# Channel products by halves with seven products (Strassen) in a second part, three pair streams, two fold buffers and plain blocks of 128 rows

## The chip, the cores and the metric

One core of one Trainium2 chip. The metric is the device time of one execution in microseconds, median of several. The profile is one execution with the hardware profiler on; its span is 1.8 us shorter than the time of that same execution (1486.8 against 1488.62 before) and some 5 us below the medians. The granted clock is the share of TensorE's full clock that it was given, as the profile shows it. TensorE is called PE below, VectorE DVE, ScalarE ACT, GpSimd POOL, SyncE SP.

## The reference

```python
# attention: q, k, v of (8, 8, 576, 64), omega (128, 64)
phi(x) = exp(x @ omega.T - |x|^2 / 2 - rowmax) / sqrt(128)
num    = phi(q) @ (phi(k).T @ v);  den = phi(q) . sum(phi(k)) + 1e-6
x      = num / den, heads side by side         # (8, 576, 512)
# Fourier mixing and channel products
u   = x + real(fft(fft(x, axis=1), axis=2))
un  = (u - mean) / sqrt(var + 1e-6)            # over the last axis
out = u + relu(un @ w_ch1) @ w_ch2             # 512 -> 2048 -> 512
```

All of it is float32 (the weights arrive as float64). There are 4608 rows of 512.

## The kernel before

The program is a set of streams (generators) whose steps name an engine, an assumed duration, what they wait for and which buffers they take. A list scheduler runs them against a model of the engines before anything runs on the chip, and so fixes the order of instructions on every engine. On the chip each engine works through its own list in that order and waits where its data are not there. Two pair streams do the attention of two heads each, `mixing` does the Fourier part of a batch, `channels` the two channel products. All run in one list, so the channel products fill TensorE's gaps in the first 700 us; work that does so is called filler below.

```python
def folds(n, which, dur, **more):            # n = 0 on VectorE, 1 on GpSimd
    yield Step(which, dur[0], **more)        # more: take=("half",)
    eng, op = ((nc.vector, ALU.add), (nc.gpsimd, ALU.subtract))[n]
    h = fft.tile([CP, NC3, DM], F32, name="half", tag="half")    # one buffer
    eng.tensor_tensor(out=h[:], in0=lo, in1=hi, op=op)
    ...                                      # three more operations
    yield Step(which, 0.2, makes=("fold", b, n), give=("half",))
...
yield from folds(0, DVE, (1.8, 1.0, 0.56), take=("half",))
yield Fork(folds(1, POOL, (3.5, 1.85, 1.1), take=("half",)))
...                                          # yp: y takes "half" too
def pairs(start):
    for n in range(start, B * NP, 2):
        if n >= 3 * NP:
            yield Step(NONE, late=PACE)      # 25 us
        yield from attn(n)
...
Listing(buffers).run([first(), loads(), norms(), mixing(),
                      pairs(0), pairs(1), channels(), weights()])
```

In the profiles `pp`, `kvp`, `tps`, `ndp` are TensorE's attention work, `yp` and `ab` its Fourier work, `tp` the transposes of the normed rows, `hp` and `op` the first and second channel product. `kq` and `vd` are loads of k, q and v; `half` and `fold` the folds ahead of `yp` (VectorE adds rows and columns of x to their mirror images, GpSimd subtracts them); `nmx` and `e` the softmax.

## Time and profile before

| | before |
|---|---|
| time, median | 1491.95 us (1490.35 to 1494.24, 4 runs) |
| TensorE busy | 1413.0 of 1486.8 us |
| channel products, of that | 1008.6 us |
| up to 697.7 us (all streams mixed) | TensorE busy 627.5, idle 70.2 |
| after 697.7 us | channel products only, 83.79 us for 384 rows |

The table of stretches tells where TensorE waits. Its columns are the stretch, its length, busy time of PE, PE load, DVE, ACT and POOL with instruction counts, the granted clock, the DMA share and GB/s.

```profile
0.00:250.00 250.00, 190.95 (x1333) 156.88 (x1334) 160.03 (x327) 118.85 (x348) 93.94 (x105) 0.88 0.58 160
250.00:697.70 447.70, 436.58 (x2723) 320.13 (x2722) 182.80 (x446) 182.88 (x564) 97.17 (x98) 0.99 0.39 104
697.70:1486.80 789.10, 785.45 (x2189) 407.26 (x2187) 56.06 (x126) 84.06 (x170) 15.21 (x24) 1.00 0.08 28
```

From 250 us on TensorE is hardly ever idle.

### The profile page before, as it was taken

What the parts mean: (1) busy time and instruction counts of PE and PEld (TensorE: products, weight loads), DVE (VectorE), ACT (ScalarE), POOL (GpSimd) and SP (SyncE); (2) the same over time, 40 slices, a digit from 0 to 9 for tenths busy, and PEclk for the clock granted to TensorE, in tenths of its full rate; (3) what the DMA queues carried; (4) which work ended last, traced back from release to release, by engine and by line L of the source; (5) the groups of instructions that cost most, each with busy time, mean ns of one, the idle gap of its engine ahead of it and who ended that gap; (6) DMA issues with size and microseconds to landing.
All of it is one profiled execution on the core that took longest, in us unless ns stands there. A gap on an engine that the chain in (4) does not pass through costs nothing.

```text
span 1486.8 us, 16157 instructions
## 1 busy us (share of the span) xinstructions
PE 1413.0 (95%) x6241; PEld 884.3 (59%) x6241; DVE 398.9 (27%) x898; ACT 385.8 (26%) x1081; POOL 206.3 (14%) x226
## 2 busy tenths in 40 slices
PE   8666888899999999999999999999999999999999
PEld 7555666677777777766454545455454545555453
DVE  6756585534344353513100101010100101010000
ACT  7543534435344544321010101111010101111010
POOL 3334354221203030322000000000000000000000
PEclk9878989999999999999999999999999999999999
DMA  8745634444433535222101001010101001010101
GB/s 220 189 126 157 180 93 137 129 118 119 112 100 97 137 82 148 60 64 75 50 0 46 19 29 36 15 50 9 56 0 39 25 29 36 15 50 6 37 0 36
DMA packets 133987, 108.60 MB, mean 73 GB/s; under 512 B 99236, under 2 KB 99492, under 8 KB 133910
## 3 DMA queue, kind: packets, MB, share of 16 engines
q1 hardware_dynamic: 127766, 86.06, 21.2%
q0 software_dynamic: 6144, 21.50, 4.5%
q8 instruction: 50, 0.82, 0.2%
q14 instruction: 27, 0.22, 0.0%
HBM read 79.22 MB, written 33.03 MB: 75 GB/s over the span
## 4 chain that ended last, share of the span: by engine, by line
PE 80%; DMA 11%; DVE 3%; POOL 2%; issue 2%; ACT 1%; SPq 1%; DVEq 0%; POOLq 0%; ACTq 0%
PE hp L724 31%; PE op L747 31%; PE pp L398 5%; PE kvp L420 3%; DMA x<-xb 3%; DMA xb<-xs 2%; PE tps L337 2%; PE yp L555 2%; DMA raw<-in_moe_w_ch_dram 2%; PE ndp L457 1%; DMA xs<-xo 1%; PE ab L581 1%; PE tp L681 1%; DVE half L515 1%; ACT e L366 1%
## 5 line engine op out<-in xcount | busy, mean ns | idle before, releaser
L747 PE MATMUL op<-w,ht 128*128 128x512 f32 x1152 | 505.7, 593 | 0.0
L724 PE MATMUL hp<-unT,w 128*128 128x384 f32 x1536 | 502.9, 486 | 0.0
L724 PEld LDWEIGHTS hp<-unT,w 128*128 128x128 f32 x1536 | 289.7, 190 | 197.4 <-issue 4.3
L747 PEld LDWEIGHTS op<-w,ht 128*128 128x128 f32 x1152 | 215.3, 190 | 248.5 <-issue 244.9
L710 ACT ACTIVATE ht<-hp 128x384 f32<-128x384 f32 x188 | 92.5, 492 | 683.4 <-PE hp L724 683.4
L761 DVE TENSOR_TENSOR ur<-ur,op 128x512 f32<-128x512 f32 x36 | 24.7, 687 | 711.2 <-PE op L747 711.2
L366 ACT ACTIVATE e<-pp,nmx 128x128 f32<-128x128 f32 x576 | 154.8, 421 | 108.1 <-DVE nmx L354 108.0
L398 PE MATMUL pp<-om,kqT 128*128 128x256 f32 x576 | 142.9, 400 | 34.2 <-DVE xo L472 13.3
L398 PEld LDWEIGHTS pp<-om,kqT 128*128 128x128 f32 x576 | 112.8, 201 | 60.7 <-issue 19.1
L675 POOL TENSOR_TENSOR rstd<-rstd,mhalf 128x1 f32<-128x1 f32 x36 | 23.0, 645 | 657.2 <-DVE rstd L673 657.2
L354 DVE TENSOR_REDUCE nmx<-pp 128x4 f32<-128x512 f32 (+1 forms) x160 | 95.9, 631 | 65.8 <-PE pp L398 54.4
L420 PE MATMUL kvp<-vd,e 128*128 128x130 f32 x576 | 82.0, 300 | 7.8 <-ACT e L366 6.9
L420 PEld LDWEIGHTS kvp<-vd,e 128*128 128x128 f32 x576 | 79.5, 212 | 15.2 <-ACT e L366 10.1
L515 POOL TENSOR_TENSOR half<-x 97x1536 f32<-97x1536 f32 x8 | 28.5, 3565 | 207.3 <-DVE rden L468 138.7
L286 POOL TENSOR_TENSOR w<-w,raw 128x512 f32<-128x512 f32 x32 | 44.0, 1380 | 95.3 <-DVE raw L284 82.5
L343 ACT ACTIVATE kqT<-tps 128x512 f32<-128x512 f32 (+1 forms) x96 | 42.5, 510 | 42.5 <-PE tps L337 42.2
L343 ACT ACTIVATE qeT<-tps 128x512 f32<-128x512 f32 (+1 forms) x96 | 41.1, 512 | 33.5 <-PE tps L337 33.5
L457 PE MATMUL ndp<-kv,qeT 128*64 128x65 f32 x1152 | 41.0, 227 | 7.9 <-DVE kv L432 7.6
L457 PEld LDWEIGHTS ndp<-kv,qeT 128*64 128x64 f32 x1152 | 36.9, 140 | 19.4 <-issue 17.7
L337 PE MATMUL tps<-ident,kq 128*128 128x128 f32 x288 | 42.2, 284 | 6.0 <-DMA kq<-in_k_dram 3.6
L685 ACT ACTIVATE unT<-tp 128x512 f32<-128x512 f32 x36 | 19.5, 601 | 99.8 <-PE tp L681 99.8
L604 DVE SCALAR_TENSOR_TENSOR bmp<-ab,bmp 97x65 f32<-97x65 f32 x96 | 25.0, 326 | 71.2 <-ACT bmp L599 70.2
(59 smaller groups left out, 750.4 us busy)
## 6 DMA issues: line engine op xcount, KB each, us to landing
raw<-in_moe_w_ch_dram POOLq DMA_DIRECT2D x32, 512.0 KB, 5.1
kq<-in_k_dram SPq DMA_DIRECT2D x32, 288.0 KB
kq<-in_q_dram SPq DMA_DIRECT2D x32, 288.0 KB
vd<-in_v_dram SPq DMA_DIRECT2D x64, 144.0 KB
xs<-xo SPq DMA_DIRECT2D x64, 144.0 KB
out_dram<-ur SPq DMA_DIRECT2D x36, 256.0 KB
u<-us SPq DMA_DIRECT2D x32, 256.0 KB
ur<-us SPq DMA_DIRECT2D x32, 256.0 KB
```

What stands on the lines that cost most here:

```text
L286: nc.gpsimd.tensor_tensor(out=dst, in0=dst, in1=lof, op=ALU.add)
L337: nc.tensor.transpose(ps[:, (j - j0) * 128 : (j - j0 + 1) * 128], src(j), ident[:])
L343: nc.scalar.activation(out=dst[:, j0:j1, :].rearrange("q c p -> q (c p)"), in_=ps[:, 0 : 128 * (j1 - j0)], func=AF.Copy,)
L354: nc.vector.tensor_reduce(nmx[:, 0:num], ps[:, 0 : MF * num].rearrange("p (c m) -> p c m", m=MF), axis=AX.X, op=ALU.max, negate=True,)
L366: nc.scalar.activation(out=e[:, c, :], in_=ps[:, MF * c : MF * c + MF], func=AF.Exp, bias=nmx[:, c : c + 1],)
L398: nc.tensor.matmul(ps[:, 256 * j : 256 * j + 256], lhsT=kqT[:, 2 * t + j, :], rhs=om2[:].rearrange("p i m -> p (i m)"),)
L420: nc.tensor.matmul(kvp[:, 0 : 2 * (D + 1)], lhsT=feature(r), rhs=vds[n % NV][:, r, :], start=(r == 0), stop=(r == R - 1),)
L457: nc.tensor.matmul(ndp[r // 5][cols, (D + 1) * (r % 5) : (D + 1) * (r % 5 + 1)], lhsT=qeT[:, r, cols], rhs=kvs[0][:, i, :],)
L515: eng.tensor_tensor(out=h[:], in0=lo, in1=hi, op=op)
L710: nc.scalar.activation(out=ht[:], in_=hp[:], func=AF.Relu)
L724: nc.tensor.matmul(hp[:], lhsT=w1[:, dc, 128 * fc : 128 * fc + 128], rhs=unTs[j][:, dc, :], start=(dc == 0), stop=(dc == NDC - 1),)
L747: nc.tensor.matmul(yp[:], lhsT=hs[fc][:, 128 * i : 128 * i + 128], rhs=w2[:, fc, :], start=(fc == 0), stop=(fc == NFC - 1),)
```

## The change

The intent is to save an eighth of the channel products. With each operand cut in halves, seven products and some additions replace eight products. The sums of the weights need memory, so the program is cut in two. In the first part run attention, Fourier part and 512 plain rows. In the second, with its own buffers, run the other 4096 rows in eight blocks of 512.

```diff
+    NS = 3                       # pair streams
     NV = 2                       # load buffers for k, q and for v
-    TB = 384
+    NHALF = 2                    # buffers for the folds and for y
+    TP = 128
+    NPLAIN = 4                   # plain blocks of 128 rows, first part
+    TB = 512                     # rows of a late block
...
-            h = fft.tile([CP, NC3, DM], F32, name="half", tag="half")
+            h = fft.tile([CP, NC3, DM], F32, name="half", tag="half", bufs=NHALF)
...
-    def pairs(start):
-        for n in range(start, B * NP, 2):
-            if n >= 3 * NP:
-                yield Step(NONE, late=PACE)
-            yield from attn(n)
+    def pairs(start):
+        for n in range(start, B * NP, NS):
+            yield from attn(n)
...
+    listing.run([first(), loads(), plain_norms(), mixing()]
+                + [pairs(i) for i in range(NS)] + [plain(), weights()])
+    early.close()                # the first part's memory is free
...
+    # first layer, one column group: seven products in three banks
+    product(x, lambda d: w1[:, d, f], lambda d: un[:, d, t1], True)
+    yield Fork(save("p1", x))                      # ACT copies the bank
+    product(z, lambda d: w1s[:, 0, d, f], lambda d: tt[:, 0, d, :], True)
+    yield Fork(save("p5", z))
+    product(x, lambda d: w1s[:, 1, d, f], lambda d: tt[:, 1, d, :], False)
+    ...                                            # four more
+    # relu of a sum on DVE (a custom add with clamping), sums hs on POOL
+    # second layer: the same scheme, sums added to the residual on DVE
+    listing.run([late_norms(), halves(), weight_sums()])
```

## The prediction

> **What bounds the kernel now.** I read the page's busy row and slices first, then the chain of waits in order of time, then the TensorE timeline of the steady part and of the mixed part, then the table of stretches.
>
> ```profile
> PE 1413.0 (95%) x6241; PEld 884.3 (59%) x6241; DVE 398.9 (27%) x898; ACT 385.8 (26%) x1081; POOL 206.3 (14%) x226
> ...
> PE   8666888899999999999999999999999999999999
> ...
> PEclk9878989999999999999999999999999999999999
> ...
> L747 PE MATMUL op<-w,ht 128*128 128x512 f32 x1152 | 505.7, 593 | 0.0
> L724 PE MATMUL hp<-unT,w 128*128 128x384 f32 x1536 | 502.9, 486 | 0.0
> ```
>
> TensorE (PE) is the bound. The two channel products take 505.7 + 502.9 = 1008.6 us of its 1413.0, with no idle time before them; VectorE and ScalarE are at a quarter. Only the first slices show a PE that waits.
>
> ```profile
> 697.71 32.62 PE op L747 x76
> 730.33 41.28 PE hp L724 x128
> 771.61 8.58 PE op L747 x20
> 781.50 32.62 PE op L747 x76
> ```
>
> In the chain of waits (start, duration, what) everything from 697.71 us on is channel work, 83.79 us for each 384 rows. The spacing of matmuls is 41.28/128 = 0.3225 us at 384 columns and 8.58/20 = 0.429 at 512: columns times 0.833 ns plus 2.5 ns. Each product written in the kernel is two such instructions.
>
> ```profile
> 408.19 4.05 PE L398 MATMUL pp<-om,kqT 128*128 128x256 f32 x18
> 412.07 2.18 PE L420 MATMUL kvp<-vd,e 128*128 128x130 f32 x18
> 414.09 2.75 PE L724 MATMUL hp<-unT,w 128*128 128x384 f32 x8
> ```
>
> These are the decisive lines, as the change makes all late products 256 wide. Starts are 3.88 us apart for 18 matmuls of 256 columns with weights loaded for each: 0.2156 us, again 256 x 0.833 + 2.5. Even 130 columns go at 2.02/18 = 0.112 us. So narrow matmuls keep the full rate, though one weight load is listed at 190 to 212 ns: loads overlap one another and the matmuls.
>
> ```profile
> 0.00:50.00 50.00, 36.29 (x290) 32.00 (x291) 29.84 (x64) 29.66 (x87) 16.45 (x29) 0.93 0.84 219
> 50.00:100.00 50.00, 33.56 (x279) 29.33 (x277) 28.75 (x56) 24.41 (x76) 11.57 (x11) 0.81 0.56 153
> 100.00:150.00 50.00, 36.91 (x260) 31.12 (x259) 37.24 (x85) 21.79 (x66) 23.29 (x25) 0.84 0.51 143
> 150.00:200.00 50.00, 40.69 (x237) 30.55 (x237) 31.71 (x52) 22.47 (x67) 20.94 (x17) 0.87 0.51 139
> 200.00:250.00 50.00, 43.51 (x273) 33.89 (x272) 32.47 (x75) 20.52 (x57) 21.68 (x24) 0.93 0.47 143
> ```
>
> Columns: PE, PE load, DVE, ACT, POOL busy, granted clock, DMA share, GB/s. PE idles 13.7 + 16.4 + 13.1 + 9.3 + 6.5 = 59 us here, at a clock of 0.81 to 0.93; from 250 us to the end it idles only some 12 more. What holds it, in the lists of waits of DVE (50 to 100 us), ACT (100 to 150) and PE (0 to 100); columns: total, times, longest:
>
> ```profile
> DVE half L515 <- DMA x<-xb: 12.9, 1, 12.9
> ...
> ACT e L366 <- DVE nmx L354: 14.6, 1, 14.6
> ...
> PE pp L398 <- DVE xo L472: 11.4, 1, 11.4
> ```
>
> These are one event near 84 to 99 us: DVE stands on a transfer for the Fourier part; the softmax behind it in the same queue stands too, and PE behind that.
>
> **What the Trainium skill says.** "FP8 and Floating Point Precision" under "TensorE Precision Notes" lists true FP32 as four passes through the array (H*H + H*L + L*H + L*L); the trace agrees: two instructions a product at 0.833 ns a column, which is two passes each at the 2.4 GHz of the TensorE page. "TensorE: Matmul & The Clock Gate", Part 1, "What's actually happening", says an idle window of about 3.4 us drops the clock to half; the granted 0.81 to 0.93 where PE waits, against 1.00 later, agrees. The same page under "Architectural detail: the array is 16× 32×32, not 1× 128×128" calls ACT and DVE strict FIFO; the 12.9 us wait above, passed on to the softmax, agrees. "SBUF — State Buffer", "SBUF: two separate sides", says of the port shared by VectorE and GpSimd that a two-SBUF-input VectorE operation and a GpSimd one that reads SBUF block each other. The change puts many such pairs side by side; no run here isolates it yet.
>
> **The change, part by part.** Rows 512 to 4607 (8 blocks of 512) move to a second part that starts when all attention and Fourier work is done. Each product is split in halves: seven products for eight.
>
> Late products. First layer per block: 8 column groups x 7 products x 2 matmuls = 112; second layer: 2 x 7 x 8 = 112. In 8 blocks 1792, each 2 x 0.2156 = 0.4313 us: 773 us. Before, these rows cost 82.48 us per 384 rows without transposes, so 880 us. Gain 107 us, one eighth.
>
> Their side work, per pair of column groups (2 x 14 x 0.4313 = 12.1 us of PE): ACT 8 evictions of 256 columns at about 0.39 us (289 columns take 417 ns) = 3.1; DVE 6 adds at 0.42 (estimate from 687 ns at 512) = 2.5; POOL 8 additions at 0.74 (257 columns take 744 ns) = 5.9. All lie beside PE. A product waits for the eviction of the one before it in the same bank, but the order of instructions puts two others, 1.7 us, between them, against about 0.9 us of drain, semaphores and copy. I allow 3 us for all seams, and 112 late transposes x 0.11 = 12 us.
>
> First part. It keeps 512 rows as blocks of 128: 256 products of 128 columns x 2 x 0.109 = 56 us, and 64 of 512 columns x 2 x 0.429 = 55 us: 111, what these rows cost before too. The other work of this part I take from the kernel before: up to 697.7 us PE carried 384 hp instructions (124 us) and 1152 - 76 - 9 x 96 = 212 op instructions (91), 215 us, and idled 70; so all else took 697.7 - 215 - 70 = 412 us. (At full clock it would be 32 pairs x 9.07 + 8 Fourier stages x 10 + transposes = 375; the clock costs the rest.) Then 412 - 3 + 111 = 520, plus idle time. The start idles as before, 59 us: those waits are queues standing on DMA and a third stream stands with the others. Later, filler is 111 us where it was 215, and the deliberate pacing of pairs is gone, so the transfers of the Fourier part are less covered: 25 instead of 12. First part: 520 + 84 = 604 us. (DVE and ACT have some 325 and 290 us to do in it, so they are not the bound.)
>
> Boundary. The order of instructions shows sixteen transposes (four tiles) behind the last plain product, then the first late one, which needs the last of four differences on DVE. DVE, in order behind the last plain addition: seven weight sums (7 x 0.69 = 4.8), statistics of two tiles (2.05, by 0.69 + 0.18 + 0.15 each), POOL's power, the scaling (0.54), then the other two tiles, whose loads wait for the first tiles' buffers (about 4.5 us from issue, as for u before), with sums in between, then four differences (2.8). Laid end to end: first tiles normed at 11 to 13 us after the last plain product, second loaded at 16 to 17, normed at 22, differences at 26. So 27 us with 1 to 3 us for a cold clock.
>
> End: last addition and store, 4 us as now (1483.2 to 1486.8).
>
> Sum: 604 + 27 + 773 + 12 + 3 + 4 = 1423 us of span; timed runs stand 5 us above the profiled span (1491.7 against 1486.8): 1428.
>
> **The rivals.** First: the late products do not reach 0.2156. Each group is only four instructions with a semaphore ahead, and weights alternate between tables. At 0.23 it costs 1792 x 2 x 0.0144 = 52 us, and the time is 1480. Against it: pp also waits on semaphores every four instructions and holds the rate. For it: POOL and DVE share a port, and hs from POOL gates the second layer; yet POOL has 5.9 of 12.1 us and 6.9 us of other products to catch up in.
>
> Second: the first part becomes a chain of latencies. With little filler, PE may idle 130 us instead of 84, about 1475. For it: DVE's waits on x sum to 60.9 us over the kernel, mostly hidden behind channel products that are now gone. Against: three streams give the list more to place there.
>
> Third: three streams and the missing pacing do better than I allow, and idle falls to 45 us: 1390.
>
> Fourth: the boundary is wider, since late tiles take over early memory and must wait for its last readers and transfers: the order shows the first late load waiting on all queues. 45 us instead of 27: 1446.
>
> **Range and chances.** The 107 us of the products are near certain if the rate holds; 27 go to the boundary, 3 to seams, 13 to idle time of a first part with less filler: 64 remain, 4%. The uncertainty is mostly the idle time of the first part (plus or minus 30) and the boundary (plus or minus 10): 1392 to 1465. Faster by over 2% means under 1461.9: 0.85; within 2%: 0.12; slower: 0.03.
>
> **What would show it.** The late part should run 98 to 99 us per 512 rows (against 111.7 before), with matmuls of 256 columns 0.216 us apart and PE busy throughout; the last plain product should end near 604 us, with one PE gap of about 25 us behind it whose releaser is DVE; POOL should be near half busy in the first layer, without PE waiting on it. I am wrong on the rate if the late part takes over 830 us, and on the first part if it ends outside 570 to 640.

## The result, and the profile after

The changed kernel is correct and slower: 1535.48 us median (1532.04 to 1539.56, 4 runs) against 1491.95. The ratio is 1.0292 (95% interval 1.0261 to 1.0322). Ratios here are the mean time of one kernel's runs over that of the other's runs of the same rounds, so not quite the ratio of the medians. The predicted 1428 and its range of 1392 to 1465 were wrong.

The page of the changed kernel, its busy row and two rows of slices (38 us each):

```profile
PE 1333.8 (87%) x7777; PEld 1153.0 (75%) x7777; DVE 594.3 (39%) x1254; ACT 405.2 (26%) x1189; POOL 402.1 (26%) x482
...
PE   6656886687968859667799999999999999999999
...
PEclk8869988898989979789899999999999999999999
```

TensorE has 79 us less to do (1413.0 to 1333.8), yet the span grew by 43. The low digits, which ended in the eighth slice before, now go on into the twentieth. Stretches of the changed kernel, to be set against those of before:

```profile
0.00:250.00 250.00, 184.34 (x1407) 160.66 (x1407) 150.25 (x300) 117.80 (x358) 83.34 (x90) 0.85 0.54 146
250.00:719.00 469.00, 358.24 (x2658) 297.20 (x2658) 226.90 (x457) 170.02 (x543) 122.58 (x104) 0.88 0.37 98
719.00:760.00 41.00, 24.43 (x107) 20.39 (x107) 31.52 (x61) 7.77 (x18) 8.51 (x12) 0.79 0.25 75
760.00:1530.20 770.20, 766.77 (x3608) 674.76 (x3606) 185.59 (x437) 109.66 (x270) 187.64 (x276) 1.00 0.09 30
```

Between 250 and 719 us TensorE is idle for 469 - 358 = 111 us, and its clock is 0.88 where it was 0.99. From 760 us on it is idle for 3 us, which is the end.

The late part is as planned. Two starts of a block, one block apart, in the TensorE timeline:

```profile
839.21 1.03 PE L901 MATMUL sx<-unT,w 128*128 128x256 f32 x4
...
937.66 1.03 PE L901 MATMUL sx<-unT,w 128*128 128x256 f32 x4
```

That is 98.45 us for 512 rows, where 83.79 us for 384 rows had made 111.7 before. The first late product starts at 738.92 us, where the prediction had 604 + 27 = 631. From there to the last matmul's end it takes 788 us, and 788 had been predicted (773 + 12 + 3). So the whole error of 107 us in the span lies ahead of the first late product.

The boundary, in the TensorE timeline (the last plain product ends at 719.1):

```profile
717.67 1.45 PE L769 MATMUL op<-w,ht 128*128 128x512 f32 x3
729.26 2.02 PE L688 MATMUL tp<-ident,u 128*128 128x128 f32 x8 [10.14 <-DVE u L684]
736.96 2.17 PE L688 MATMUL tp<-ident,u 128*128 128x128 f32 x8 [5.67 <-DVE u L684]
738.92 2.64 PE L901 MATMUL sx<-unT,w 128*128 128x256 f32 x8
741.40 0.81 PE L901 MATMUL sz<-tt,w1s 128*128 128x256 f32 x3
```

It takes 20 us, not 27. TensorE waits for VectorE's scaling of the rows (u), as foreseen, but the first product (sx) needs only the transposed rows; sz is the first that uses the differences.

What TensorE waited for in the changed kernel (us in total, times, longest):

```profile
PE yp L567 <- DVE fold L538: 48.1, 5, 15.9
PE tps L349 <- DMA kq<-in_k_dram: 36.0, 7, 18.2
PE yp L567 <- DVE nmx L366: 29.3, 3, 16.0
PE tp L688 <- DVE u L684: 28.6, 5, 11.5
PE kvp L432 <- DMA vd<-in_v_dram: 23.4, 5, 13.2
```

Before, yp waited for 0.6 us in all. Now it waits for 48.1 + 29.3 = 77, and everything behind it in TensorE's order waits too. The folds of one batch show why. First before, then after (start, duration, what):

```profile
94.22 1.76 DVE L515 TENSOR_TENSOR half<-x 97x1536 f32<-97x1536 f32 x1 [12.94 <-DMA x<-xb]
96.01 0.95 DVE L517 TENSOR_TENSOR half<-half 97x765 f32<-97x765 f32 x1
97.00 1.03 DVE L526 TENSOR_TENSOR fold<-half 97x384 f32<-97x384 f32 x2
97.95 0.16 DVE L534 COPY mid<-half 97x3 f32<-97x3 f32 x1
...
98.20 3.42 POOL L515 TENSOR_TENSOR half<-x 97x1536 f32<-97x1536 f32 x1 [20.37 <-DVE rden L468]
```

```profile
95.97 1.76 DVE L527 TENSOR_TENSOR half<-x 97x1536 f32<-97x1536 f32 x1 [0.31 <-DMA x<-xb]
96.02 5.01 POOL L527 TENSOR_TENSOR half<-x 97x1536 f32<-97x1536 f32 x1 [18.95 <-DMA x<-xb]
97.77 4.07 DVE L529 TENSOR_TENSOR half<-half 97x765 f32<-97x765 f32 x1
...
101.10 2.40 POOL L529 TENSOR_TENSOR half<-half 97x765 f32<-97x765 f32 x1
101.87 3.31 DVE L538 TENSOR_TENSOR fold<-half 97x384 f32<-97x384 f32 x2
103.58 2.46 POOL L538 TENSOR_TENSOR fold<-half 97x384 f32<-97x384 f32 x2
...
105.11 0.96 DVE L546 COPY mid<-half 97x3 f32<-97x3 f32 x1
```

With one buffer GpSimd begins when VectorE has ended. With two, both begin at 96.0 and take turns. GpSimd's first operation lasts 5.01 us for 3.42, as VectorE's first 1.76 us go ahead of it. VectorE's second then stands until GpSimd's ends at 101.03, and ends 0.8 us later, about its own length. VectorE is held 10.1 us instead of 3.9 in each of eight batches, while GpSimd's folds end 10.3 us after the data are there instead of 11.9. The durations agree with the exclusive lock of "SBUF — State Buffer", "SBUF: two separate sides": whichever operation starts first has the shared port pair for the whole instruction. The prediction cited that section for the second part, where it did little harm (VectorE's custom additions took at most 0.425 us; of GpSimd's 256 sums one took 1.05 us, the others at most 0.73), and did not apply it to the folds.

### The profile page after: what moved, and what is told of

Its sections match the earlier page's. It is cut to its first block, busy times and chain, and to the rows that moved or that the text cites. A ratio compares the mean times of both kernels' runs of the same rounds, so it can differ in the third digit from the quotient of the medians.

```text
span 1530.2 us, 20250 instructions
## 1 busy us (share of the span) xinstructions
PE 1333.8 (87%) x7777; PEld 1153.0 (75%) x7777; DVE 594.3 (39%) x1254; ACT 405.2 (26%) x1189; POOL 402.1 (26%) x482
## 4 chain that ended last, share of the span: by engine, by line
PE 70%; DMA 13%; DVE 8%; SPq 3%; issue 3%; ACT 2%; POOL 1%; DVEq 0%; POOLq 0%
PE sx L988 14%; PE sx L901 14%; PE sz L988 7%; PE sz L901 7%; PE sy L988 4%; PE yp L567 4%; PE sy L901 3%; PE pp L410 3%; DMA x<-xb 3%; PE kvp L432 3%; DMA xs<-xo 2%; PE tps L349 2%; DMA xb<-xs 2%; PE hp L746 2%; DVE half L529 2%
## 5 line engine op out<-in xcount | busy, mean ns | idle before, releaser
L961 POOL TENSOR_TENSOR hs<-ht,ht 128x256 f32<-128x256 f32 x64 | 46.7, 729 | 455.6 <-DVE ht L888 455.6
L915 ACT ACTIVATE s<-sx 128x256 f32<-128x256 f32 x128 | 49.2, 384 | 328.0 <-PE sx L901 328.0
L901 PE MATMUL sx<-unT,w 128*128 128x256 f32 x512 | 131.8, 381 | 0.0
L567 PE MATMUL yp<-cs_sb,fold 97*128 97x289 f32 x96 | 45.9, 657 | 81.8 <-DVE fold L538 48.1
L988 PE MATMUL sx<-w,ht 128*128 128x256 f32 x512 | 114.4, 379 | 0.0
L901 PEld LDWEIGHTS sx<-unT,w 128*128 128x128 f32 x512 | 97.9, 191 | 13.4
L988 PEld LDWEIGHTS sx<-w,ht 128*128 128x128 f32 x512 | 96.7, 190 | 12.9
L432 PEld LDWEIGHTS kvp<-vd,e 128*128 128x128 f32 x576 | 78.3, 211 | 34.9 <-issue 23.5
L567 PEld LDWEIGHTS yp<-cs_sb,fold 97*128 97x128 f32 x96 | 29.4, 319 | 95.8 <-issue 34.3
L349 PEld LDWEIGHTS tps<-ident,kq 128*128 128x128 f32 x288 | 36.7, 155 | 46.2 <-issue 41.3
L901 PE MATMUL sx<-tt,w 128*128 128x256 f32 x256 | 65.7, 380 | 0.8 <-DVE ht L888 0.8
```

Of the source, the lines that this page charges most:

```text
L349: nc.tensor.transpose(ps[:, (j - j0) * 128 : (j - j0 + 1) * 128], src(j), ident[:])
L432: nc.tensor.matmul(kvp[:, 0 : 2 * (D + 1)], lhsT=feature(r), rhs=vds[n % NV][:, r, :], start=(r == 0), stop=(r == R - 1),)
L567: nc.tensor.matmul(yp[:, 0:NK], lhsT=fold[:, c, n, :], rhs=tab[:, c, :], start=(c == 0), stop=(c == NC3 - 1),)
L901: nc.tensor.matmul(ps[:, 0:HT], lhsT=left(dc), rhs=right(dc), start=start and dc == 0, stop=(dc == D2 - 1), skip_group_check=True,)
L915: nc.scalar.activation(out=s[:], in_=ps[:, 0:HT], func=AF.Copy)
L961: nc.gpsimd.tensor_tensor(out=o, in0=l, in1=r, op=op)
```

## The experiments

The first set of theories was:
- Collision: the two fold buffers cost, by the lock and by the place in the order that the list, which assumes no collision, gives to yp.
- Streams: the third pair stream costs.
- Filler: the channel products of before had covered waiting that nothing covers now.

The runs in one table. The last two columns are from the profiles: start of the first late product, and TensorE's idle time ahead of it. Rounds of one kernel before differed a little (medians 1491.95 to 1497.1), so the ratio is the safer number.

| run | time, us | ratio to before (95%) | first late product, us | idle ahead, us |
|---|---|---|---|---|
| the change | 1535.5 | 1.029 (1.026, 1.032) | 738.9 | 192 |
| half1 | 1485.3 | 0.993 (0.989, 0.997) | 689.5 | 154 |
| honest | 1524.3 | 1.020 (1.018, 1.022) | 729.2 | 183 |
| yown | 1501.9 | 1.006 (1.002, 1.009) | 708.1 | 162 |
| ns2 | 1502.4 | 1.006 (1.003, 1.009) | 709.1 | 163 |
| ns2_half1 | 1467.5 | 0.980 (0.977, 0.984) | 676.3 | 131 |
| ns2_half1_pace | 1463.2 | 0.978 (0.975, 0.980) | 674.4 | 133 |
| ns2_half1_pace_hold | 1464.4 | 0.980 (0.976, 0.983) | 675.9 | 125 |
| half1_kq3 | 1507.7 | 1.009 (1.007, 1.011) | 710.3 | 174 |
| half1_nv3 | 1480.9 | 0.990 (0.988, 0.993) | 687.3 | 146 |
| half1_nv3_p8 | 1485.0 | 0.994 (0.991, 0.997) | 788.8 | 132 |
| ns2_half1_pace_p8 | 1445.0 | 0.967 (0.965, 0.969) | 745.4 | 95 |
| ns2_half1_p8 | 1443.6 | 0.964 (0.961, 0.967) | 752.9 | 106 |
| ns2_half1_pace_p12 | 1457.6 | 0.977 (0.971, 0.982) | 863.1 | 97 |
| b_late | 1611.4 | 1.079 (1.075, 1.083) | 602.1 | 155 |

In the runs with p8 and p12 more rows are done ahead of the first late product, so their starts are not to be compared with the others. In b_late it is the first channel product. All gave the right result.

**One fold buffer (half1).**

```diff
-    NHALF = 2
+    NHALF = 1
```

> The changed kernel with one buffer for the half folds instead of two, so that VectorE's and GpSimd's folds run one after the other again. Collision theory (the two folds block each other, 10.1 us on VectorE instead of 4.0, and the order list, which counts on 4.1, puts the Fourier matmuls about 8 us too early, in front of everything else on TensorE; 77 us of TensorE idle time in front of yp): VectorE's fold is back at 4 us, idle time before yp under 20 us, time 1455 to 1480. Streams theory (three pair streams on two load buffers, 59 us of waiting on kq and vd): within 10 us of the changed kernel's 1535. Filler theory (the gaps were always there, the removed channel products had filled them): within 20 us of 1535, the idle time moving from yp to other lines.

It gave 50 us, from 1535.5 to 1485.3. VectorE's folds are short again; one group of half1 (busy us, mean ns, idle before):

```profile
L529 DVE TENSOR_TENSOR half<-half 97x765 f32<-97x765 f32 x8 | 7.6, 954 | 0.2
```

This one took 4055 ns on average in the changed kernel. The waits of TensorE in half1 no longer name yp, except for 2.0 us, but those on the loads of k stay:

```profile
PE tps L349 <- DMA kq<-in_k_dram: 44.6, 9, 18.8
...
PE kvp L432 <- DMA vd<-in_v_dram: 11.5, 4, 7.6
```

The time came out 5 us above the expected 1455 to 1480, so of the 77 us in front of yp 50 came out in the time. Streams and filler had both expected about 1535 and missed. The collision theory holds for a large part of the loss, not for all.

**True durations for the list (honest), and a buffer of its own for y (yown).** One buffer changes two things: the folds follow each other, and y, which shares their buffers, must wait for the second fold, so that yp is listed later. These two runs try to take them apart; yown also changes y's buffer in the list, in lines left out here.

```diff
-        yield from folds(0, DVE, (1.8, 1.0, 0.56), take=("half",))
-        yield Fork(folds(1, POOL, (3.5, 1.85, 1.1), take=("half",)))
+        yield from folds(0, DVE, (1.8, 4.05, 1.7), take=("half",))      # honest
+        yield Fork(folds(1, POOL, (4.9, 2.4, 1.25), take=("half",)))
```

> The changed kernel with two fold buffers, but the durations that the order list assumes for the folds set to what the trace shows (VectorE 1.8, 4.05, 1.7, 1.7; GpSimd 4.9, 2.4, 1.25, 1.25). The collision stays, only the order of instructions changes. Collision theory, in its part about the order: the Fourier matmuls come later in TensorE's order, idle time before yp falls from 77 us to under 35, time 1475 to 1505. If the collision costs only by holding VectorE, no change (1525 to 1540). Streams and filler theories: 1520 to 1540.

```diff
-    NHALF = 2
+    NHALF = 1                                                           # yown
...
-                y = fft.tile([128, 4, NK], F32, name="y", tag="half", bufs=NHALF)
+                y = fft.tile([128, 4, NK], F32, name="y", tag="y", bufs=1)
```

> The changed kernel (three streams) with the folds back in one buffer, but the Fourier products' result y in a buffer of its own. Only the folds' running at the same time is taken away; the second buffer stays for y. If it is the collision: as half1, 1475 to 1490. If half1 gained because y's reuse of the buffer put yp in a better place: over 1500.

With true durations and the collision kept, 1524.3: 11 us, not the 30 to 60 expected. With the collision gone and yp free to be listed early, 1501.9, between the two outcomes. Taken at face value, some 34 of half1's 50 us come from the end of the collision (1535.5 to 1501.9) and some 17 from the later place of yp that the shared buffer enforces (1501.9 to 1485.3). This split is a reading and not shown, as each edit rearranges the whole list. In yown yp still waits 42 us:

```profile
PE yp L567 <- DVE fold L538: 25.3, 5, 11.4
PE yp L567 <- DVE nmx L366: 16.7, 2, 10.5
```

**Two streams (ns2, ns2_half1), and the old hold on the pairs (ns2_half1_pace).**

```diff
-    NS = 3
+    NS = 2
...
         for n in range(start, B * NP, NS):
+            if n >= 3 * NP:                     # only in ns2_half1_pace
+                yield Step(NONE, late=25.0)
             yield from attn(n)
```

> The changed kernel with two pair streams instead of three (two fold buffers stay). Streams theory: the waits on kq and vd (59 us) fall to under 15 us, time 1480 to 1495. Collision theory: those waits only follow from the late Fourier matmuls; time 1520 to 1550 and the idle time before yp stays above 50 us. Filler theory: longer, 1540 to 1570, as there is less work to put in the gaps.

> Two pair streams and one fold buffer, without the holding back of pairs. If the two costs found (50 us for two fold buffers, 33 us for three streams) add up, 1455 to 1470, and the holding back is worth nothing (under 10 us against ns2_half1_pace at 1463). If the holding back of pairs was what helped there, 1480 or more.

> The first part as the kernel before has it (two streams, one fold buffer, each pair from the twelfth on held back 25 us in the order list), with only the 512 plain rows to fill it. Filler theory: it is the removed filler that costs; the first part keeps its old length of about 690 us although 100 us of channel work is gone from it, time 1500 to 1530. Collision theory: the first part ends near 600 to 620 us and the time is 1430 to 1450.

Two streams are better by 33 us with two fold buffers and by 18 with one. In the same way one fold buffer is worth 50 us with three streams and 35 with two: the two costs overlap. No theory had foreseen ns2: streams expected 1480 to 1495, collision 1520 to 1550 and filler 1540 to 1570, and 1502 came out. Collision's yp waits did stay, at 43.5 + 27.8 us in ns2. The hold is worth nothing measurable (1463 against 1467). Most important, with both edits undone the time is still 1463, between the 1430 to 1450 of the collision theory and the 1500 to 1530 of the filler theory. Something is left that none of the edits undone here carries.

**The kernel before without its filler (b_late).** This edits the kernel before, not the changed one.

```diff
     def channels():
+        yield Step(NONE, after=(("us", B - 1),))      # all Fourier work done
         for j in range(NTB):
             yield from mlp(j)
```

> The kernel before with nothing of the change in it, except that its channel products start only when all attention and Fourier work is done: the first part without any filler. It measures what the prediction took from the sums of the kernel before, 412 us of other work plus idle time. If my 84 us of idle time for the first part were right for the pattern of waits and only the change's own edits spoiled it, the first part is 480 to 510 us and the time 1495 to 1525. If the channel products had hidden far more waiting than the profile of before showed as idle, the first part is 530 us or more and the time 1545 or more.

The time is 1611.4 us and the first channel product starts at 602.1. The stretches of b_late:

```profile
0.00:250.00 250.00, 176.26 (x1336) 152.97 (x1337) 153.44 (x321) 120.65 (x364) 88.02 (x100) 0.84 0.62 166
250.00:602.12 352.12, 271.29 (x2087) 233.35 (x2086) 165.69 (x391) 155.50 (x496) 91.17 (x86) 0.86 0.43 108
```

Attention and Fourier work alone take 602 us, of which TensorE is busy for 447.5 and idle for 154.6. In the kernel before, 215 us of channel work went into the same stretch and made it 697.7 us long, so 602 + 215 - 698 = 119 us of it were covered. The profile of before had shown only 70 us of idle time there, because that is what was left when the gaps had been filled. The clock adds to it: 0.85 here, against 0.95 up to 697.7 us before, and the same work is 447.5 us busy rather than the 412 taken from before (the 576 instructions of pp alone 151.0 against 142.9). b_late keeps the hold on the pairs, which had been set with filler there; what it is worth without any was not tested.

**More plain rows (p8, p12), and the same rows placed later (hold).** If filler is short, more plain rows should help, though 512 rows cost TensorE 111 us in plain form and 98 in the late one.

```diff
-    NPLAIN = 4
+    NPLAIN = 8        # 1024 rows, 7 late blocks; p12: 12, 1536 rows, 6 blocks
...
     def plain():                                     # only in hold
         for j in range(NPLAIN):
+            if j >= 2:
+                yield Step(NONE, after=(("x", B - 1, 1),))
             yield from plain_of(j)
```

> The best so far with 1024 plain rows instead of 512 (seven late blocks of 512 instead of eight). Filler theory: 512 rows more in plain form cost 13 us of TensorE time (111 against 98), but cover the 19 us before the last Fourier matmuls and most of the 23.5 us before the late norms: 1435 to 1455. If idle time does not come from a lack of filler: 1476, that is 13 us longer than without.

> The same with 1536 plain rows. The order of instructions shows several plain blocks behind the last Fourier matmuls, where they fill nothing, so it should be 8 to 13 us longer than with 1024 rows: 1445 to 1465. If more filler always helps: under 1440.

> ns2_half1_pace_p8 without the holding back of pairs. As it was worth nothing with 512 plain rows (1467 against 1463), 1440 to 1455; if it sets where the filler falls, 1460 or more.

> The best first part (two streams, one fold buffer, pairs held back) with 512 plain rows, the last two blocks of 128 of which are held until the last batch's Fourier input is on its way, so that they cover the wait before the last Fourier matmuls and the wait before the late norms (19 and 24 us of idle time in ns2_half1_pace). If that placement is what 1024 plain rows bought: 1425 to 1445. If not: as ns2_half1_pace, 1463.

With 1024 plain rows the time is 1445, 18 us better in spite of 13 us more TensorE work. Idle time ahead of the late part falls from 133 to 95 us. Some 13 of these 38 us lie at the boundary: in ns2_half1_pace, where the plain blocks end early, 33 us pass from the last Fourier matmul (641.6) to the first late product; with 1024 plain rows 20 us pass from the last plain product (725.7). With 1536 it is 1458, and idle time is no less (97 us): the additional blocks come after the gaps and fill nothing. Even with 1024 the last plain product ends 80 us after the last Fourier matmul. Without the hold on the pairs the time is the same within the noise, 1444, the best and 3.6% faster than before.

Holding two of the four blocks back did not help (1464). It closed the gap in front of the last Fourier matmuls and shortened the wait at the boundary, and opened others. TensorE's waits in ns2_half1_pace, then in ns2_half1_pace_hold:

```profile
PE tp L688 <- DVE u L684: 39.2, 5, 23.5
PE pp L410 <- DVE xo L484: 22.3, 3, 13.4
PE yp L567 <- DVE fold L538: 19.3, 1, 19.3
PE tps L349 <- DMA kq<-in_k_dram: 17.3, 7, 4.3
...
PE kvp L432 <- ACT e L378: 4.7, 5, 2.6
```

```profile
PE tp L688 <- DVE u L684: 28.2, 5, 10.0
PE tps L349 <- DMA kq<-in_k_dram: 25.0, 7, 7.5
PE pp L410 <- DVE xo L484: 17.6, 2, 12.9
PE kvp L432 <- ACT e L378: 14.9, 7, 5.8
```

The 19.3 us are gone and 23.5 became 10.0, but waits on k and on the softmax are up by 8 and 10 us. So the expectation that placement was what p8 bought failed. That it was the amount of filler is the likely reading: with 111 us for more than 130 us of gaps, moving it moves the gap. Only this one other placement was tried.

**Load buffers for the third stream (half1_kq3, half1_nv3, half1_nv3_p8).** In half1 the queue that issues the transfers stood for 127.6 us on loads of v whose buffer was not yet free, and stood before everything behind them.

```diff
-    ld = early.enter_context(tc.tile_pool(name="ld", bufs=NV))
+    ld = early.enter_context(tc.tile_pool(name="ld", bufs=3))           # kq3
...
-    NV = 2
+    NV = 3                              # nv3: for k, q and v; p8: NPLAIN = 8
-            ur = mlpp.tile([P, DM], F32, name="ur", tag="ur", bufs=2)
+            ur = mlpp.tile([P, DM], F32, name="ur", tag="ur", bufs=1)   # nv3
```

> Three streams with one fold buffer and a third load buffer for k and q. If three streams cost because they share two load buffers (44.6 us of waits on kq in half1), those waits fall under 15 us and the time to 1450 to 1465. If the buffers are not it (the loads stand in one queue behind other transfers that wait), the waits stay or move to v and the time stays at 1475 to 1490.

> half1 (three streams, one fold buffer) with three load buffers for k and q and three for v, so that each stream has its own (one buffer less for the residual rows of the plain blocks, to make room). If three streams cost because the in-order transfer queue stands on the v load until a buffer is free (some 128 us of that wait in half1, against 44 in all for two streams) and everything behind it stands too, that wait falls under 40 us, TensorE's waits on kq and vd (56 us) under 20, and the time is 1455 to 1470, as with two streams. If it is not the buffers: 1480 or more.

> The same with 1024 plain rows. If the buffers were it, three streams now do as well as the two of ns2_half1_pace_p8: 1430 to 1455. If not: 1465 or more.

A third buffer for k and q alone made it 22 us worse, which neither outcome had: the waits on k fell only to 32.5 us, and those of tp on u rose from 41.4 to 70.7. With three of each, the queue's wait fell as expected. The wait of the queue on v, first in half1, then in half1_nv3:

```profile
SPq L242 <- PE tps L349: 127.6, 14, 17.9
```

```profile
SPq L242 <- PE tps L349: 22.3, 3, 10.9
```

But the time improved by only 4 us, to 1480.9, no more than the noise, and with more plain rows it did not gain at all (1485.0), where two streams gained 18 to 24. TensorE no longer waited for v, but still 30.0 us for k, and other waits moved to what VectorE hands over:

```profile
PE pp L410 <- DVE xo L484: 19.9, 2, 17.6
PE ndp L469 <- DVE kv L444: 16.4, 2, 15.3
```

So a shortage of load buffers is not the main reason, and why the third stream costs stays open. That it costs shows in each pair of runs (33, 18 and, with p8, 41 us, where the load and residual buffers differ too). Every such edit rearranges the whole list, however, and half1_kq3, which only adds a buffer, came out 22 us slower. I take only the sign as shown.

## Why the prediction was wrong

By its own steps:

- **Late products, right.** 1792 products at 0.4313 us, transposes and seams made 788 us, and 788 was measured; a block takes 98.45 us against the 98 to 99 predicted. The rate of narrow matmuls, read from pp, holds. The custom addition took 0.425 us for the 0.42 estimated and POOL's sums 0.73 for 0.74. POOL was busy 24.4 us per block, about half of the first layer, and TensorE waited 0.8 us on these engines in all.
- **Boundary, right in kind, 7 us too long.** 20 us for 27; the prediction had put the differences on the path of the first product, which does not need them.
- **Plain rows, nearly right.** The 512 instructions of hp are 63.7 us busy and the 128 of op 57.6, where 56 and 55 us at full clock had been reckoned.
- **First part, wrong: this is the failed step.** It was put as "all else took 697.7 - 215 - 70 = 412 us ... Then 412 - 3 + 111 = 520, plus idle time ... 25 instead of 12", 604 us. Measured is 719, outside the 570 to 640 that the prediction had named as its sign of being wrong here. TensorE is 542.6 us busy where 520 had been reckoned, and 176.4 idle where 84 had been set: 65.7 in the first 250 us (59 set) and 110.8 after them (25 set). So "25 instead of 12" is the term that failed most, by 86 of the 115 us; 23 are busy time, at a granted clock of 0.87 up to 719 us. Two errors lie behind it, and the first cannot be undone by undoing the edits:
  1. Idle time of a filled stretch was taken as the waiting of the work in it. b_late measures what should have been used: 602 us without filler, 447.5 busy and 154.6 idle, where my sum amounts to 412 + 84 = 496. Not all of those 106 us were lost, since the plain blocks cover some. With the edits undone (ns2_half1) the first late product starts at 676 instead of the predicted 631, 45 us late; about half of that is longer busy time (545.6 us up to there, where some 522 had been reckoned) and half idle time.
  2. Edits of the change that I did not price at all. The second fold buffer is not mentioned in the prediction: 49 us of start (738.9 to 689.5). In the trace VectorE and GpSimd block each other; how much of the 49 us that makes, and how much the order, is not shown. The third stream I counted as neutral or good: 13 us of start with one fold buffer (689.5 to 676.3), 18 us of time.
  45 + 49 + 13 = 107 us, the error of the sum. The parts add up because each is measured from the one before; undone in the other order, the third stream is 30 us and the fold buffer 33.
- **Rivals.** The second came nearest. It named the first part as a chain of latencies with 130 us idle (176 were measured) and 1475 us in all. Its cause was right in kind ("mostly hidden behind channel products that are now gone"); I gave it too little weight, as the amount hidden was never estimated, and "three streams give the list more to place there", set against it, had the wrong sign. The first rival (the rate) and the fourth (a wider boundary) fell. So did the third: three streams did worse, not better.

What settles the sign: late products saved about 106 of the 107 us foreseen, less a boundary of 20. The separation cost the cover that these same products had given, and the new buffers and stream added some 60 us of waiting.

## What to carry to other kernels

Idle time in a well filled stretch is not the waiting time of its work. Before moving filler out of a stretch, run the stretch without it, one edit that holds the filler back, and price the move from that. When a second buffer lets VectorE and GpSimd work on SBUF operands at the same time, check their durations: here VectorE's chain grew by 6 us, while GpSimd's ended only 1.6 us sooner, and the list that places TensorE's work had been told of no such delay. A saving of one eighth in products is worth trying where the products stand alone; there it came in full.

## What the Trainium skill lacked or had wrong

- "SBUF — State Buffer" has the lock of the shared port right, and these runs agree with it. It gives no case of two chains that take turns for their whole length: VectorE 10.1 us for 3.9, GpSimd's first operation 5.01 us for 3.42, and even a copy of 3 elements a partition 0.96 us for 0.16.
- "TensorE: Matmul & The Clock Gate" has no figures for float32 products. Here each is two instructions, started N x 0.833 + 2.5 ns apart at N from 256 to 512 and full clock, and new weights for each add nothing to that even at 130 columns (0.112 us between starts), though a load is listed at 190 to 212 ns, where the page's formula, columns / 1.2, gives 107 ns.
- The same page tells of the clock after an idle window and of single matmul kernels that lose it again and again; it has no figure for a mix of work like this one. With TensorE busy for 74% of 602 us (b_late) the granted clock averaged 0.85, and work estimated at 412 us took 447.5.
- No page has the time of a custom VectorE addition with one operand in PSUM: 0.425 us for 128x256, as an ordinary addition (0.421), and with no longer case among 192 (0.408 to 0.425 us) while GpSimd's sums ran in the same stretch.
